# Attention followed by an MLP on one core: engine orders searched with another rule for ties between GpSimd's masks and VectorE's 16-bit sums

## The chip, the cores and the metric

The kernel runs on one core of a Trainium2 chip. A core has four compute engines that matter here: TensorE (PE, matmuls), VectorE (DVE), ScalarE (ACT) and GpSimd (POOL); SyncE (SP) issues transfers. Each engine works through its own list of instructions in order and waits on semaphores for the others. The metric is the device time in microseconds (us) of one execution; the figure for a kernel is the median of several runs.

## The reference

Attention with a few extra "beacon" keys that every query may see, then an MLP with a gated activation:

```python
B, H, S, Nb, D = 8, 8, 576, 16, 64
k_all = concat([beacon_k, k], axis=2)            # 592 keys
scores = q @ k_all.T / sqrt(D)                   # per batch and head
scores[causal] = -1e9                            # beacon keys are never masked
a = exp(scores - max); a /= a.sum(-1) + 1e-9
x = (a @ v_all).transpose(0, 2, 1, 3).reshape(4608, 512)
h = x @ w_in                                     # 512 -> 2048
out = (h * sigmoid(1.702 * h)) @ w_out           # 2048 -> 512, float32
```

## The kernel before

**Attention.** The 64 pairs of batch and head are worked in 16 sets of four heads, two sets to a batch. The score matrix is computed transposed, keys on the partitions, and only where the causal mask leaves something. It is cut into 60 chunks of up to 512 columns for four heads at once, so that a chunk fills four PSUM banks. For chunk i, the operation `qk` of the plan (L571 for sets 0 to 7, whose queries and keys are transposed by DVE; L560 for sets 8 to 15, whose transposed copies come by a transposing DMA from a staged 16-bit copy, L489 and L493) makes the scores; `exp` (L583, ACT) writes their exponentials as 16-bit numbers into E. There is one score tile, so chunk i+1 waits for the exponentials of chunk i. `mask` (L601, POOL, `affine_select`; for the first sets some of them on DVE, L594) zeroes the part of a block above the diagonal. `zadd` (L619, DVE, 16-bit sums) adds the key blocks of E up into zs, from which PE forms the softmax denominators with a matmul by ones. `av` (L659, PE) are the matmuls of attention: the first index after the set says which half of the head dimension is formed, 2 stands for the denominators. `z1` and `z2` (L669, L675, L680, DVE) transpose the denominators and invert them, `norm` (L697, DVE) multiplies and writes x, transposed, into xT.

**MLP.** Its tokens go in ten groups, two of 256 and eight of 512. The first layer is `m1` (L721), or, for some groups, a fast scheme with seven products instead of eight, whose pieces `f` (L926) are combined by ACT (`seed` L936, `keep7` L942) and DVE (`sum` L945) and activated at L951. The second layer is plain (`m2`, L767, copied from PSUM by `evac`, L780) for the first two groups; from group 2 on it is also a scheme of seven products (L839), with sums of its right sides on DVE in 16 bit (`s`, through a helper, L787), `half` (ACT, L852) and `join` (DVE, L855) behind it, and stores on SP (L863, L870). The weights' own sums (wsum, t, in SF and tB) and those of x (xsum, in tiles that the profile names sig) also run through L787. All these 16-bit sums are DVE instructions that read E, x, weights or activations from SBUF.

**Order.** Nothing about the order is found at run time. The program first lists about 1,740 operations with their dependencies. A literal table ORDER then gives for each engine the sequence of its operations, by number, and a literal list BANK the PSUM bank of each tile, in the order in which the tiles are first named. PSUM has eight banks: four form a ring that av, m1, m2, f and the products share; the other four hold the score tile or, in the phases between, more of the ring's tiles. A tile may open in a bank only when the operations that close the bank's last tile (norm, gelu, evac, half, join and their like) are done.

`Plan.run` (from L184) walks these lists: at each step it looks at the first operation left of every engine, works out from estimated durations and latencies when it could start, and takes the earliest. The result is the order in which instructions are emitted to the program; the sequence on each engine is that of ORDER in any case. The plan models that DVE's 16-bit sums and POOL's masks use a shared port: an operation carries port 1 (a DVE operation whose name is in HELD: s, zadd, xsum, wsum, t, mask, bk) or port 2 (a POOL mask), and does not start before the planned end of the last operation with the other port:

```python
                if o.port:
                    t = max(t, held[3 - o.port])
                if first is None or t < first[0]:
                    first = t, e, i
```

Engines are looked at in the order PE, ACT, DVE, POOL, SP, so that with equal starts DVE's sum is placed before POOL's mask, and the mask is then held behind it.

ORDER and BANK were made outside of this program, by a search over such plans. At the start PE runs warm-up matmuls (L1525) while the first loads arrive.

Of the kernel before, what the change touches and what calls it, by code (L numbers as in the profile page):

```python
# [18 lines left out]
        126, 136, 162, 165, 235, 129, 147, 131, 150, 152, 240, 168, 171, 242, 249, 174, 194, 245, 177, 197, 266,  # L19
        200, 203, 206, 209, 275, 256, 212, 215, 254, 277, 284, 252, 259, 261, 287, 280, 180, 225, 181, 226, 416,  # L20
        291, 289, 227, 294, 296, 419, 182, 187, 183, 422, 228, 188, 189, 190, 429, 320, 302, 310, 316, 308, 328,
        306, 332, 314, 304, 322, 318, 312, 324, 326, 330, 342, 343, 438, 447, 218, 219, 220, 221, 450, 351, 352,
        353, 344, 367, 476, 362, 345, 368, 363, 369, 364, 618, 370, 372, 373, 354, 374, 365, 621, 375, 441, 445,
        486, 443, 627, 386, 387, 491, 493, 646, 489, 388, 389, 503, 379, 648, 380, 381, 505, 382, 507, 519, 535,
        541, 509, 525, 537, 511, 539, 512, 515, 543, 544, 521, 523, 547, 553, 527, 557, 528, 531, 551, 555, 576,
        567, 568, 651, 637, 577, 578, 569, 579, 570, 592, 593, 816, 597, 598, 587, 594, 588, 819, 589, 590, 595,
        599, 660, 822, 640, 644, 642, 665, 830, 604, 605, 600, 663, 667, 848, 606, 607, 611, 673, 612, 851, 613,
        614, 677, 679, 882, 681, 682, 675, 685, 689, 695, 711, 705, 727, 709, 707, 723, 713, 714, 721, 693, 691,
        717, 839, 697, 698, 725, 746, 701, 737, 747, 748, 1020, 892, 844, 738, 739, 740, 749, 757, 758, 1023,
        842, 846, 897, 899, 895, 1030, 759, 762, 774, 775, 763, 1049, 776, 767, 764, 768, 760, 1051, 765, 769,  # L30
        770, 777, 905, 1054, 781, 907, 782, 783, 909, 921, 937, 784, 911, 955, 923, 925, 913, 914, 941, 939,
        927, 930, 929, 943, 917, 946, 945, 933, 957, 949, 959, 953, 969, 970, 971, 1219, 1063, 1040, 972, 989,
        978, 979, 980, 990, 981, 1222, 991, 992, 1045, 1043, 1066, 1225, 1068, 1070, 1047, 994, 1233, 995, 996,
        997, 1076, 999, 1251, 1000, 1001, 1002, 1006, 1007, 1254, 1013, 1008, 1009, 1014, 1080, 1285, 1078,
        1015, 1084, 1016, 1085, 1092, 1082, 1124, 1108, 1094, 1096, 1110, 1088, 1112, 1098, 1114, 1128, 1101,
        1100, 1116, 1117, 1126, 1104, 1120, 1295, 1242, 1130, 1149, 1140, 1141, 1431, 1142, 1150, 1151, 1245,
        1249, 1152, 1143, 1434, 1247, 1300, 1302, 1298, 1441, 1160, 1161, 1162, 1163, 1165, 1460, 1166, 1177,
        1178, 1167, 1170, 1462, 1168, 1179, 1171, 1172, 1308, 1173, 1465, 1180, 1310, 1184, 1312, 1185, 1324,
        1186, 1187, 1340, 1314, 1326, 1328, 1342, 1330, 1316, 1317, 1356, 1344, 1320, 1332, 1333, 1358, 1360,
        1451, 1474, 1336, 1365, 1364, 1362, 1346, 1454, 1456, 1349, 1348, 1368, 1458, 1479, 1481, 1477, 1352,  # L40
        1380, 1381, 1487, 1503, 1389, 1390, 1489, 1391, 1505, 1491, 1507, 1382, 1392, 1509, 1511, 1383, 1495,
        1512, 1493, 1400, 1515, 1496, 1405, 1406, 1407, 1519, 1401, 1499, 1535, 1402, 1525, 1408, 1403, 1521,
        1523, 1539, 1537, 1410, 1411, 1527, 1412, 1413, 1528, 1531, 1541, 1543, 1559, 1568, 1569, 1560, 1544,
        1570, 1547, 1417, 1561, 1424, 1425, 1614, 1426, 1630, 1418, 1419, 1618, 1420, 1634, 1427, 1632, 1616,
        1596, 1562, 1579, 1597, 1580, 1598, 1571, 1599, 1581, 1638, 1582, 1636, 1623, 1584, 1585, 1620, 1639,
        1642, 1586, 1622, 1589, 1646, 1590, 1587, 1591, 1626, 1592, 1662, 1650, 1648, 1603, 1604, 1666, 1668,
        1605, 1606, 1652, 1654, 1664, 1655, 1670, 1671, 1658, 1686, 1674, 1687, 1695, 1696, 1706, 1688, 1689,
        1711, 1697, 1712, 1716, 1713, 1698, 1714, 1707, 1708, 1709, 1717, 1718, 1719, 1720, 1725, 1726, 1727,
# [4 lines left out]
        172, 243, 175, 246, 178, 195, 198, 267, 201, 204, 207, 210, 276, 213, 216, 278, 281, 417, 420, 184, 423,  # L53
        191, 431, 430, 229, 303, 311, 317, 333, 309, 329, 321, 315, 307, 305, 319, 313, 323, 325, 327, 331, 448,
        222, 451, 478, 477, 350, 619, 622, 628, 629, 647, 504, 649, 506, 536, 508, 510, 538, 542, 540, 514, 520,
        526, 516, 522, 524, 546, 548, 554, 550, 518, 530, 532, 558, 552, 534, 556, 652, 575, 817, 820, 823, 832,
        831, 849, 674, 852, 678, 680, 884, 883, 684, 686, 706, 676, 688, 712, 710, 708, 728, 690, 696, 716, 720,
        694, 722, 718, 724, 692, 700, 704, 726, 702, 1021, 745, 1024, 1031, 1032, 1050, 1052, 906, 1055, 908,
        922, 938, 910, 956, 912, 924, 926, 916, 940, 928, 942, 920, 944, 932, 918, 936, 934, 958, 952, 948, 950,
        960, 954, 1220, 977, 1223, 1226, 1234, 1235, 1252, 1077, 1255, 1081, 1286, 1287, 1079, 1093, 1083, 1109,  # L60
        1125, 1087, 1111, 1089, 1095, 1097, 1113, 1099, 1129, 1115, 1091, 1107, 1103, 1127, 1121, 1119, 1123,
        1105, 1131, 1432, 1148, 1435, 1442, 1443, 1461, 1463, 1309, 1466, 1311, 1325, 1341, 1315, 1313, 1327,
        1343, 1331, 1329, 1319, 1357, 1321, 1323, 1335, 1361, 1359, 1337, 1339, 1363, 1345, 1347, 1367, 1351,
        1355, 1369, 1488, 1353, 1504, 1490, 1371, 1506, 1492, 1508, 1510, 1388, 1494, 1514, 1518, 1516, 1498,
        1500, 1536, 1520, 1522, 1526, 1524, 1538, 1540, 1530, 1502, 1534, 1542, 1532, 1550, 1546, 1548, 1615,
        1631, 1617, 1633, 1619, 1635, 1567, 1637, 1621, 1641, 1643, 1629, 1645, 1647, 1663, 1627, 1625, 1651,
        1649, 1667, 1653, 1669, 1657, 1665, 1661, 1659, 1677, 1675, 1673, 1694, 1743,
# [3 lines left out]
        232, 233, 127, 157, 128, 161, 164, 130, 148, 167, 413, 149, 132, 151, 153, 170, 263, 250, 173, 265, 264,  # L71
        176, 179, 196, 251, 199, 202, 205, 208, 257, 211, 258, 214, 255, 285, 253, 217, 286, 262, 415, 414, 288,
        260, 426, 292, 290, 293, 297, 495, 427, 295, 298, 428, 496, 434, 497, 299, 300, 435, 475, 436, 335, 437,
        334, 339, 336, 340, 338, 439, 337, 624, 347, 473, 474, 341, 440, 301, 346, 355, 348, 356, 482, 626, 349,
        625, 483, 484, 359, 366, 371, 485, 442, 376, 487, 488, 444, 357, 358, 492, 494, 446, 490, 499, 390, 500,
        501, 502, 498, 383, 513, 633, 545, 517, 656, 549, 529, 634, 533, 561, 635, 559, 565, 636, 563, 560, 564,
        562, 638, 571, 573, 566, 582, 639, 584, 574, 572, 657, 658, 659, 591, 596, 661, 662, 641, 581, 645, 666,
        643, 580, 601, 668, 664, 669, 583, 608, 670, 671, 672, 615, 888, 683, 835, 836, 687, 837, 838, 729, 733,
        715, 719, 889, 840, 699, 703, 890, 891, 841, 732, 730, 734, 731, 735, 741, 893, 845, 742, 894, 754, 843,
        743, 847, 750, 751, 898, 896, 1036, 900, 901, 902, 736, 744, 752, 761, 753, 766, 771, 778, 903, 904,  # L80
        1059, 1037, 785, 1060, 915, 919, 931, 935, 951, 947, 1061, 961, 962, 965, 1038, 966, 963, 967, 1039,
        1062, 973, 964, 968, 1041, 976, 974, 975, 1042, 1064, 986, 1065, 993, 1067, 1044, 982, 1046, 1071, 984,
        1072, 985, 1069, 1073, 983, 1074, 998, 1075, 1048, 1003, 1238, 1010, 1239, 1017, 1240, 1291, 1086, 1241,
        1090, 1292, 1293, 1294, 1106, 1102, 1118, 1122, 1132, 1243, 1244, 1136, 1133, 1134, 1135, 1296, 1137,
        1297, 1144, 1138, 1250, 1145, 1246, 1154, 1157, 1139, 1146, 1248, 1299, 1147, 1156, 1304, 1447, 1303,
        1164, 1155, 1305, 1301, 1306, 1448, 1449, 1307, 1169, 1174, 1153, 1181, 1450, 1188, 1470, 1471, 1318,
        1472, 1473, 1322, 1334, 1338, 1372, 1452, 1453, 1475, 1476, 1366, 1455, 1457, 1350, 1376, 1373, 1459,
        1480, 1354, 1478, 1370, 1483, 1374, 1484, 1485, 1486, 1384, 1393, 1482, 1375, 1378, 1379, 1377, 1513,
# [1473 lines left out]
```

## Time and profile before

| | |
|---|---|
| median of 3 runs | 320.81 us (320.31 to 320.88) |
| profiled execution | 321.22 us |
| its span, from the first to the last instruction | 319.4 us |
| mean granted TensorE clock in the span | 0.997 |
| moved by DMA | 33.51 MB in 112522 packets |

How to read the profile's lines: an instruction group has a line number of the program, an engine, the operation, the tile written and the tile read with partitions x elements, the count after an x, the busy time and the mean of one in ns, and then the idle time of the engine just ahead of the group with what ended it. A row of the timeline has start, duration, engine, line, operation, tiles and count; several like instructions in a row stand as one with their count, and a bracket tells how long the engine was idle before. The duration of a row of matmuls holds the modelled drain of the last one, so rows of PE overlap by some tenths, and the price of a matmul is read from start to start. A row of the windows has the stretch, its length, and for each engine the busy time in it. In the waits, "PE s L560 <- DMA qT<-qD: 0.6, 1, 0.6" means that PE, at line 560 on tile s, waited 0.6 us in total, once, and at most 0.6, for that transfer.

### The profile page before, as it was taken

Reading aid. Unit: us, or ns where it says so; the run is one execution under the profiler, and the core shown is the slowest. Engines: PE = TensorE matmul, PEld = TensorE weight load, DVE = VectorE, ACT = ScalarE, POOL = GpSimd, SP = SyncE. Lnnn points to the kernel's source line nnn. Section 1 sums busy time; section 2 is a strip of 40 time slices with the busy share of each in tenths; the row PEclk is TensorE's granted clock in tenths of the full one; section 3 lists DMA queues with packets and bytes.
Section 4 is the critical chain, followed back from the end, with each engine's and each line's share of the span. In section 5 each row is a group of like instructions: output and inputs, shape, how many; then the busy total and the mean of one; then the engine's idle time right before and its main releaser. Section 6 shows DMA issues by size and latency. Waiting matters only on the chain.

```text
span 319.4 us, 9295 instructions
## 1 busy us (share of the span) xinstructions
PE 309.9 (97%) x3947; PEld 232.2 (73%) x3947; DVE 255.3 (80%) x497; ACT 231.9 (73%) x309; POOL 136.7 (43%) x186
## 2 busy tenths in 40 slices
PE   6999999999999999989999999999999999999994
PEld 2567774445777777767778777777788888888884
DVE  5777988795999589897998799689958984776773
ACT  1778884677758987699869986898779687544820
POOL 8769558791848902595368204830350000000000
PEclk9999999999999999999999999999999999999998
DMA  7999999999999994599299903990036000120202
GB/s 122 178 202 191 147 192 168 138 190 95 88 87 111 192 108 92 112 159 161 17 129 151 203 0 44 155 152 30 3 23 146 2 3 2 66 68 34 101 33 101
DMA packets 112522, 33.51 MB, mean 105 GB/s; under 512 B 97504, under 2 KB 109920, under 8 KB 112480
## 3 DMA queue, kind: packets, MB, share of 16 engines
q0 software_dynamic: 83008, 18.55, 66.4%
q1 hardware_dynamic: 29264, 14.28, 19.4%
q8 instruction: 31, 0.51, 0.7%
q14 instruction: 11, 0.09, 0.1%
q10 hardware_dynamic: 208, 0.07, 0.1%
HBM read 37.22 MB, written 14.22 MB: 161 GB/s over the span
## 4 chain that ended last, share of the span: by engine, by line
PE 88%; ACT 5%; DVE 2%; DMA 2%; issue 1%; SPq 0%; DVEq 0%; ACTq 0%
PE u L839 29%; PE u L926 20%; PE u L721 13%; PE u L659 9%; PE u L767 4%; PE s L571 4%; PE s L560 4%; PE u L1525 4%; ACT E L583 2%; DMA qT<-qD 2%; PE p L571 1%; DVE osb L855 1%; ACT g L951 1%; ACT L951 1%; ACT u L936 1%
## 5 line engine op out<-in xcount | busy, mean ns | idle before, releaser
L583 ACT ACTIVATE E<-s 128x2048 f16<-128x2048 f32 (+3 forms) x59 | 90.7, 1553 | 31.7 <-PE s L560 16.0
L601 POOL TENSOR_SCALAR_AFFINE_SELECT E<-E 128x512 f16<-128x512 f16 (+3 forms) x78 | 62.5, 887 | 101.6 <-ACT E L583 86.1
L839 PEld LDWEIGHTS <-g 128*128 128x128 f16 x768 | 72.7, 98 | 11.8 <-issue 0.5
L839 PE MATMUL u<-w,g 128*128 128x256 f16 x512 | 67.2, 273 | 0.0
L951 ACT ACTIVATE g<-u 128x512 f16<-128x512 f32 x96 | 53.3, 628 | 12.4 <-DVE u L945 8.5
L855 DVE SCALAR_TENSOR_TENSOR osb<-u,osb 128x512 f32<-128x512 f32 (+2 forms) x51 | 33.2, 656 | 18.5 <-PE u L839 16.3
L721 PE MATMUL u<-xT,w 128*128 128x256 f16 (+1 forms) x256 | 45.4, 326 | 0.5 <-ACT g L951 0.5
L926 PEld LDWEIGHTS <-SF 128*128 128x128 f16 x384 | 37.2, 98 | 6.5 <-issue 0.3
L926 PE MATMUL u<-sig,SF 128*128 128x256 f16 x288 | 40.1, 273 | 0.0
L721 PEld LDWEIGHTS <-w 128*128 128x128 f16 x256 | 24.2, 98 | 15.1 <-issue 1.2
L839 PE MATMUL u<-tB,g 128*128 128x256 f16 x256 | 34.8, 273 | 0.0
L475 POOL DMA_DIRECT2D vb<-in_v_dram x32 | 33.1, 1118 | 0.0
L926 PEld LDWEIGHTS <-w 128*128 128x128 f16 x288 | 28.0, 98 | 5.3 <-issue 0.7
L936 ACT ACTIVATE u<-u 128x512 f32<-128x512 f32 x48 | 27.9, 596 | 3.8 <-PE u L926 3.1
L697 DVE TENSOR_TENSOR xT<-u,rz 128x352 f16<-128x352 f32 (+6 forms) x58 | 26.3, 478 | 3.9 <-PE u L659 3.5
L787 DVE TENSOR_TENSOR g<-g 128x512 f16<-128x512 f16 x64 | 28.1, 454 | 1.6 <-PE u L839 0.9
L926 PE MATMUL u<-xT,w 128*128 128x256 f16 x192 | 28.1, 272 | 0.3 <-ACT E L583 0.2
L659 PE MATMUL u<-E,vb 128*32 128x352 f16 (+8 forms) x928 | 27.7, 263 | 0.3 <-DVE xT L697 0.2
L659 PEld LDWEIGHTS <-vb 128*32 128x32 f16 (+1 forms) x928 | 20.4, 96 | 7.2 <-issue 3.6
L619 DVE TENSOR_TENSOR zs<-zs,E 128x1344 f16<-128x1344 f16 (+2 forms) x36 | 23.8, 662 | 1.4 <-POOL E L601 0.4
L945 DVE TENSOR_TENSOR u<-u,kn 128x512 f32<-128x512 f32 x24 | 16.0, 694 | 6.8 <-ACT kn L942 3.5
L945 DVE TENSOR_TENSOR u<-u,qn 128x512 f32<-128x512 f32 x24 | 16.1, 695 | 6.5 <-PE u L926 5.3
(72 smaller groups left out, 449.3 us busy)
## 6 DMA issues: line engine op xcount, KB each, us to landing
out_dram<-osb SPq DMA_DIRECT2D x35, 256.0 KB, 3.0
vb<-in_v_dram POOLq DMA_DIRECT2D x24, 128.0 KB, 5.6
kn<-in_k_dram POOLq DMA_DIRECT2D x8, 288.0 KB, 7.3
qn<-in_q_dram POOLq DMA_DIRECT2D x8, 288.0 KB, 6.7
qD<-in_q_dram POOLq DMA_DIRECT2D x8, 288.0 KB, 6.4
kD<-in_k_dram POOLq DMA_DIRECT2D x8, 288.0 KB, 8.1
w<-in_moe_w_in_dram POOLq DMA_DIRECT2D x8, 256.0 KB, 8.5
w<-in_moe_w_out_dram POOLq DMA_DIRECT2D x4, 512.0 KB, 9.5
```

The lines of the kernel that those rows point to most:

```text
L475: nc.gpsimd.dma_start(out=t[0 : hi - lo, j, h0:h1, :], in_=v[b, h0:h1, lo:hi, :].rearrange("h n d -> n h d"),)
L583: nc.scalar.activation(out=Es[s][:, h0:h1, c0:c1], in_=sall[(i, p)][:, :, o : o + c1 - c0], func=AFT.Exp, scale=0.125,)
L601: nc.gpsimd.affine_select(out=blk, in_=blk, compare_op=ALU.is_ge, fill=0.0, base=off + (Nb if j == 0 else 0), pattern=[[0, Q], [1, w]], ch ...
L659: nc.tensor.matmul(u[32 * h : 32 * h + 32, a:e], lhs, src[0:kw, h, col : col + e - a], start=first, stop=last, skip_group_check=s >= EARLY ...
L721: nc.tensor.matmul(u[:, o + a - t0 : o + e - t0], w1t[:, kp, nt * P : (nt + 1) * P], xT[:, kp, a % XR : (e - 1) % XR + 1], start=(kp == 0 ...
L787: (nc.vector if eng == "DVE" else nc.gpsimd).tensor_tensor(out=out, in0=a, in1=b, op=op)
L839: nc.tensor.matmul(u[:, HM * mt : HM * (mt + 1)], lhs[:, n, mt * P : (mt + 1) * P], rhs[:, n, :], start=(n == 0 and (mt == 0 or apart) and ...
L855: nc.vector.scalar_tensor_tensor(out=osbs[(g, dst)][:, c0:c1], in0=rings[("p", g, p)][:, c0:c1], scalar=scale_of(g), in1=osbs[(g, src)][:, ...
L926: nc.tensor.matmul(u[:, HM * n : HM * (n + 1)], lhs[x][:, (2 * i + n) * P : (2 * i + n + 1) * P], rhs[:, x, :], start=fresh and n == 0 and ...
L936: nc.scalar.mul(out=ring_tile(dst)[:, :], in_=rings[src][:, :], mul=1.0)
L945: nc.vector.tensor_tensor(out=rings[dst][:, :], in0=rings[src][:, :], in1=p7s[(g, i)], op=ALU.add)
L951: nc.scalar.activation(out=gts[g][:, n : n + 2, HM * h : HM * (h + 1)], in_=rings[src][:, :].rearrange("p (n w) -> p n w", n=2), func=AFT. ...
```

## The change

One condition in `Plan.run` is new: where a POOL operation could start at the very moment that another engine's could, it is taken first. And the tables ORDER and BANK are replaced by ones that a search found with this rule in its plan. No instruction is added, removed or changed in shape. Of the operations in the plan, these stand at another place in their engine's list: PE 377 of 590, DVE 356 of 451, ACT 153 of 300, POOL 143 of 179, SP 39 of 71; the largest shifts are 35, 28, 17, 84 and 5 places. PE's list has 130 changes between kinds of matmul tile where it had 133; ACT's has the same 12 loads of a function table.

```diff
@@ Plan.run @@
                 if o.port:
                     t = max(t, held[3 - o.port])
-                if first is None or t < first[0]:
+                if first is None or t < first[0] or (t == first[0] and e == "POOL"):
                     first = t, e, i
@@ ORDER, some rows of PE's list (221 lines of tables in all) @@
-        126, 136, 162, 165, 235, 129, 147, 131, 150, 152, 240, 168, 171, 242, 249, 174, 194, 245, 177, 197, 266,
-        200, 203, 206, 209, 275, 256, 212, 215, 254, 277, 284, 252, 259, 261, 287, 280, 180, 225, 181, 226, 416,
...
+        126, 136, 162, 165, 235, 129, 147, 131, 150, 152, 240, 168, 171, 242, 174, 194, 245, 249, 177, 197, 266,
+        203, 200, 206, 209, 275, 256, 212, 215, 254, 277, 284, 252, 259, 261, 287, 289, 280, 225, 180, 181, 226,
...
```

In words, the places that the prediction speaks of. Score chunk 27 stands before a half of a product of group 2 (product 4) instead of after it. The value matmuls of set 7 stand directly behind chunk 32, ahead of two product pieces. On DVE, between the reciprocals of set 12 and its first norm stand twelve sums of activations instead of seven, and PE's value tiles of sets 12 and 13 take other banks. Two copies of the plain second layer (`evac`) stand on ACT ahead of two exponentials of sets 4 and 5, instead of one ahead of them and one behind. The last `zadd` of set 5 stands ahead of the last of three joins of group 2 instead of behind it. On ACT, two exponentials of sets 9 and 10 change places ahead of the activations of group 4. The new lists begin with the same sixteen PE operations as the old ones, and the last products, joins and stores stand in the same order.

188 rows, old and new, of tables (BANK, ORDER) are left out of this document.

## The prediction

> **What bounds the kernel now.** I read the page's head first, then the chain that ended last.
>
> ```profile
> span 319.4 us, 9295 instructions
> PE 309.9 (97%) x3947; PEld 232.2 (73%) x3947; DVE 255.3 (80%) x497; ACT 231.9 (73%) x309; POOL 136.7 (43%) x186
> PE 88%; ACT 5%; DVE 2%; DMA 2%; issue 1%; SPq 0%; DVEq 0%; ACTq 0%
> ```
>
> TensorE is busy 97% of the span and carries 88% of the chain. The change touches no duration, so the only stock it can draw on is the time in which PE does not run. The windows of 20 us say where that is (left out are five in which PE is busy for all 20.00 us, others up to 300, and one with 19.99).
>
> ```profile
> core 0: us, PE busy (x) PEld busy (x) DVE busy (x) ACT busy (x) POOL busy (x), PEclk, DMA share, GB/s
> 20.00:40.00 20.00, 19.24 (x391) 15.36 (x384) 17.01 (x34) 17.19 (x19) 14.00 (x23) 1.00 1.41 175
> ...
> 80.00:100.00 20.00, 19.69 (x356) 14.63 (x353) 19.34 (x34) 13.72 (x11) 13.03 (x14) 1.00 1.06 94
> 100.00:120.00 20.00, 19.89 (x200) 15.04 (x198) 15.23 (x31) 18.58 (x29) 11.83 (x13) 1.00 1.59 140
> 120.00:140.00 20.00, 19.64 (x297) 14.70 (x295) 17.95 (x36) 15.06 (x14) 10.66 (x16) 1.00 0.77 107
> 140.00:160.00 20.00, 19.30 (x256) 14.25 (x257) 17.23 (x34) 18.23 (x28) 10.77 (x12) 1.00 1.05 110
> ...
> 200.00:220.00 20.00, 19.37 (x190) 14.66 (x189) 15.43 (x24) 18.02 (x30) 8.84 (x12) 1.00 1.33 133
> ```
>
> Missing in them: 0.76 + 0.31 + 0.11 + 0.36 + 0.70 + 0.63 = 2.87 us. DVE is the next engine: 19.34 of 20 us at 80 to 100, so a reordering of DVE is what PE can feel. The waits name two of PE's idle stretches and the one large wait that stems from the masks:
>
> ```profile
> PE s L560 <- DMA qT<-qD: 0.6, 1, 0.6
> PE u L721 <- ACT g L951: 0.5, 1, 0.5
> DVE zs L619 <- POOL E L601: 2.3, 2, 1.9
> ```
>
> The masks cost DVE 2.3 us in two waits. Of PE's waits only the DMA one, 0.6 us, has nothing to do with the order on DVE or ACT: a transposed load lands late. Counted in the two lists, as many PE operations stand between the load's first possible moment and its user in the new order as in the old, so it stays.
>
> The ends do not move. The first sixteen PE operations, to about 21 us, are the same in both lists, and so are ACT's and DVE's there; the last products, joins and stores are the same too, so what lies behind PE's last work stays:
>
> ```profile
> 313.97 1.36 PE L839 MATMUL u<-w,g 128*128 128x256 f16 x11
> 315.89 0.83 SPq L870 DMA_DIRECT2D out_dram<-osb  x2
> ```
>
> PE ends at 313.97 + 1.36 = 315.33, the last stores are issued at 315.89, the span ends at 319.4.
>
> **The change, part by part.** All times below are in the profiled execution, 321.22 us, of which 319.4 is the span; it lies 0.41 above the median of the runs, 320.81, to which I add the sum at the end. 0.2% of it, 0.64 us, is about what a measurement can tell from no change.
>
> The one changed line of the planner emits nothing: it settles which engine is served first when a mask and a sum could start at the same planned moment. Each engine's list is written out, so the chip sees only the new lists and PSUM banks: 377 of 590 PE operations stand elsewhere in their list, 356 of 451 on DVE, 153 of 300 on ACT, 143 of 179 on POOL, 39 of 71 on SP. Number, kinds and ACT's table loads are equal. So I price places.
>
> First the premise, the masks:
>
> ```profile
> L601 POOL TENSOR_SCALAR_AFFINE_SELECT E<-E 128x512 f16<-128x512 f16 x42 | 37.7, 911 | 79.2 <-ACT E L583 63.7 <-issue 15.3
> L601 POOL TENSOR_SCALAR_AFFINE_SELECT E<-E x78: 357/637/3088, 17.1 to 239.7; 128x512 f16<-128x512 f16 x42, 128x320 f16<-128x320 f16 x20, 128x448 f16<-128x448 f16 x14, 128x192 f16<-128x192 f16 x2
> 60.16 1.20 POOL L601 TENSOR_SCALAR_AFFINE_SELECT E<-E 128x512 f16<-128x512 f16 x1 [2.35 <-ACT E L583]
> 60.19 1.71 DVE L787 TENSOR_TENSOR SF<-SF,w 128x1024 f16<-128x1024 f16 x2
> ...
> 203.35 1.33 DVE L619 TENSOR_TENSOR zs<-zs,E 128x1344 f16<-128x1344 f16 x1
> 203.93 1.20 POOL L601 TENSOR_SCALAR_AFFINE_SELECT E<-E 128x448 f16<-128x448 f16 x1
> ```
>
> A mask of the 512 form takes 911 ns on average where the median mask takes 637, and one took 3088: 42 x 0.27 = 11.5 us of stretching, next to 16-bit sums on DVE. At 60.16 a mask that waited during a sum ran before the next queued sum: the rule of the new plan. At 203.35 a sum begins while a first mask runs, and the second mask, queued behind it, takes 1.20 us, twice the median, and ends 0.45 after the sum: there the sum that had waited went ahead, the rule of the old plan. So the new rule describes some collisions better and others worse, and I give the better premise no gain of its own.
>
> By the Trainium skill, page "SBUF — State Buffer", section "Who interferes with whom", the port pair that DVE shares with GpSimd is an exclusive lock; an earlier section of the page gives it to whichever operation starts first, for the whole instruction. The two places above agree, and by that rule the plan that lets a mask pass a sum already waiting is wrong where the plan before was right; this is the last rival below.
>
> Switches of PE between kinds of matmul tile (scores, attention values, the rest): 133 in the old list, 130 in the new. The price from these rows, and the place of the next term:
>
> ```profile
> 98.05 1.88 ACT L583 ACTIVATE E<-s 128x2048 f16<-128x2048 f32 x1 [0.87 <-PE s L571]
> 99.21 0.60 PE L926 MATMUL u<-xT,w 128*128 128x256 f16 x4
> 99.65 0.60 PE L839 MATMUL u<-tB,g 128*128 128x256 f16 x4
> 100.18 0.63 PE L571 MATMUL s<-qT,kT 32*128 32x400 f16 x16
> ```
>
> Four equal matmuls take 99.65 - 99.21 = 0.44 us ahead of one of their kind and 100.18 - 99.65 = 0.53 ahead of scores, hence about 0.1 a switch; three fewer: **-0.3**.
>
> Chunk 27 of the scores (at 100.18) needs the score tile that the exponential of chunk 26 reads until 98.05 + 1.88 = 99.93. In the new order it stands ahead of the product at 99.65, so PE gets there at 99.65 and waits about **+0.28**; the product then runs behind it at no loss. Below nothing it cannot go, and if ACT is late by more, so is the wait.
>
> Attention values of set 7 (131.32 here):
>
> ```profile
> 128.87 1.69 DVE L697 TENSOR_TENSOR xT<-u,rz 128x96 f16<-128x96 f32 x6
> 129.91 1.05 PE L839 MATMUL u<-tB,g 128*128 128x256 f16 x8
> 131.32 0.92 PE L659 MATMUL u<-E,vb 128*32 128x224 f16 x28
> ```
>
> They now stand directly behind chunk 32 at 129.90, 131.32 - 129.90 = 1.42 us earlier. Their PSUM banks are freed by the norms of set 6, which end at 128.87 + 1.69 = 130.56. Priced 0 to 130.56 - 129.90 = 0.66; the new list also lets DVE take some of these norms earlier, so about half: **+0.3**.
>
> Sets 12 and 13:
>
> ```profile
> 219.51 1.08 DVE L787 TENSOR_TENSOR sA<-g 128x512 f16<-128x512 f16 x3
> 222.90 0.53 DVE L697 TENSOR_TENSOR xT<-u,rz 128x352 f16<-128x352 f32 x1
> 224.31 1.88 PE L659 MATMUL u<-E,vb 128*32 128x352 f16 x57
> ```
>
> Between the reciprocals of set 12 and its first norm (222.90) the old list has 7 sums of the products' right sides, the new one 12. A sum takes about 0.33 from start to start (the three at 219.51 reach 220.51), so the norm comes 5 x 0.33 = 1.65 later. PE's user of its bank started at 224.31, 224.31 - (222.90 + 0.53) = 0.88 after it. That leaves 1.65 - 0.88 = 0.77 at most; the new list, however, hands that user a bank freed by ACT and only later users the norm's, so 0 to 0.77, the middle: **+0.4**.
>
> The first layer of group 2:
>
> ```profile
> 61.72 0.60 ACT L780 ACTIVATE osb<-u 128x512 f32<-128x512 f32 x1 [1.63 <-PE u L767]
> 62.38 1.94 ACT L583 ACTIVATE E<-s 128x1536 f16<-128x1536 f32 x2
> ```
>
> Two copies from PSUM, 0.60 each, now both stand before the two exponentials of 62.38; in the old list the second follows them. The exponentials start about 0.5 later, the masks and sums behind them too, while the bank freed by the copy comes 0.5 sooner or more. The window from 60 to 80 us has no idle PE now, so little of either reaches it: between -0.2 and +0.3, **+0.1**.
>
> Denominators of set 5:
>
> ```profile
> 90.86 2.18 DVE L855 SCALAR_TENSOR_TENSOR osb<-u,osb 128x512 f32<-128x512 f32 x3
> 92.96 0.32 DVE L619 TENSOR_TENSOR zs<-zs,E 128x320 f16<-128x320 f16 x1
> 93.33 0.38 PE L659 MATMUL u<-zs,ones 128*32 128x288 f16 x8 [0.21 <-DVE zs L619]
> ```
>
> PE waits 0.21 for the last sum, which follows three joins. In the new list it is ahead of the last join: the wait goes, **-0.2**, and the join, 0.7 later, frees its bank for nobody near.
>
> ACT's order around groups 3 and 4 touches PE's 0.5 us behind the activation of L951: the two exponentials before it change places, and the sum behind which it stood has one DVE sum less ahead of it. But the table load before it stays where it is: 0 to -0.5, **-0.1**.
>
> SP's and POOL's transfers move by few places (39 of SP's 71, by at most 5). Their cover, PE's work between the score chunks, is the same, so nothing; uncovered, the row of 0.6 us above is the price of one.
>
> Sum: -0.3 + 0.28 + 0.3 + 0.4 + 0.1 - 0.2 - 0.1 = +0.48, taken as +0.5.
>
> **The rivals.** *Slower: the DVE order of sets 7 and 12 at its full price.* The banks come free at the old pace and PE stands at both: -0.3 + 0.28 + 0.66 + 0.77 + 0.3 = +1.7, none of the small gains: 322.5. It decides once the first norm of set 12 ends over 0.88 us later than now relative to PE. For it: DVE is the second busiest engine and the PE order is tight there. Against: the banks were dealt anew with that very order.
>
> *Faster: the new order closes idle stretches.* Of 2.87 us, 0.6 stays; half of the other 2.27 goes, with the switches: -1.1 - 0.3 = -1.4: 319.4. For it: every stretch but one hangs on DVE's or ACT's order. Against: the idle time lies in six pieces under 0.8 us, and the places that I can follow show as many new tight spots as old ones loosened.
>
> *Slower by the lock: whoever waited first goes on.* The new order counts on masks passing sums that the chip does not let pass. One more DVE wait like the longest of the waits above, 1.9 us, where PE needs the sum at once, as at 93.33: +1.9, 322.7. Against: 1.9 us of that wait cost PE nothing in the old order.
>
> *The change does nothing of its own.* That the rule only reshuffles ties and every move is covered gives -0.3 to 0, inside the first case's range.
>
> **How the numbers follow.** No change that can be told, at 320.81 + 0.5 = 321.3: 0.40, with its own range from 320.2 to 322.0 (the terms at their low ends, -0.3 + 0.28 - 0.2 - 0.2 - 0.5 = -0.9, seldom all at once; the high ends are the first rival); 0.08 of this lies above +0.64 and 0.03 below -0.64. Full price: 0.26. Faster: 0.26. Lock: 0.08. So faster 0.03 + 0.26 = 0.29, same 0.40 - 0.11 = 0.29, slower 0.08 + 0.26 + 0.08 = 0.42. The range for 8 in 10 reaches from 319.2, a little under the faster case, to 323.1, a little over the lock's: the faster case left out below 319.2 holds about 0.1, and so do the two slower ones above 323.1. The time is that of the likeliest case, **321.3**.
>
> **What would show it right or wrong.** Right: the score chunk near 99.9 waits about 0.3 us for ACT; the attention values of set 7 wait up to 0.66 for L697; a wait of PE for L697 at 223 to 227; no wait for the sum at 93.3; the DMA wait near 204 still 0.6. Wrong: windows from 20 to 220 us with under 1.5 us missing (faster), or any PE wait over 1 us for DVE (the lock or the full price), or a later first matmul or longer tail, which I hold equal.

## The result, and the profile after

The changed kernel took 319.63 us (median of 7 runs), the kernel before 320.90 beside it: a ratio of 0.9955 (95% interval 0.9940 to 0.9970). Run again later beside the kernel before it was 319.55 against 320.73: 0.9970 (0.9957 to 0.9983). It is faster, by 1.2 to 1.3 us between the medians, where the prediction had 0.5 us slower. The first profile of it fell in a slow execution, with a granted TensorE clock of 0.949, so the lines here are of a second profile of the same program at the full clock (319.32 us, first experiment).

The head of its page, with busy times and the shares of the chain:

```profile
span 317.6 us, 9305 instructions
PE 309.4 (97%) x3947; PEld 232.6 (73%) x3947; DVE 247.2 (78%) x497; ACT 232.9 (73%) x309; POOL 135.5 (43%) x186
PE 64%; ACT 3%; DVE 2%; issue 1%; DVEq 0%; ACTq 0%
```

PE's work is as long as it was (309.4 for 309.9), DVE's is 8 us shorter, and little of that reaches PE, as the windows of 20 us say, in the same columns and stretches as before. (Of the 8 us, 5 lie in the 16-bit sums of L787 and L619, whose records add up to 115.9 us for 121.1. So DVE's sums are stretched less under the new lists, whether by the new rule or not no run shows.)

```profile
20.00:40.00 20.00, 19.70 (x395) 15.76 (x388) 16.91 (x34) 18.01 (x21) 14.77 (x25) 1.00 1.32 164
...
80.00:100.00 20.00, 19.39 (x354) 13.95 (x356) 19.16 (x35) 13.92 (x12) 11.54 (x12) 1.00 1.26 111
100.00:120.00 20.00, 19.99 (x204) 15.51 (x192) 15.13 (x30) 18.93 (x30) 10.25 (x15) 1.00 0.98 112
120.00:140.00 20.00, 19.43 (x305) 14.69 (x294) 17.20 (x36) 15.17 (x14) 12.82 (x18) 1.00 0.84 125
140.00:160.00 20.00, 19.51 (x276) 14.43 (x277) 16.61 (x36) 17.79 (x27) 11.35 (x13) 1.00 1.53 129
...
200.00:220.00 20.00, 19.97 (x199) 15.03 (x197) 15.82 (x30) 18.07 (x30) 6.82 (x9) 1.00 0.45 80
```

These miss 0.30 + 0.61 + 0.01 + 0.57 + 0.49 + 0.03 = 2.01 us where before missed 2.87. The largest part of the difference is one stretch, 200 to 220: 0.03 for 0.63. The stretch from 20 to 40, with 0.30 for 0.76, holds a stall that differs from execution to execution (below), and the others trade with each other. A second part lies behind PE's last matmul, in the timelines of DVE and SP there. First before, then after:

```profile
315.37 0.82 DVE L855 SCALAR_TENSOR_TENSOR osb<-u,osb 128x128 f32<-128x128 f32 x3 [1.05 <-PE u L839]
```

```profile
312.13 1.91 PE L839 MATMUL u<-w,g 128*128 128x256 f16 x16
313.21 0.42 DVE L855 SCALAR_TENSOR_TENSOR osb<-u,osb 128x256 f32<-128x256 f32 x1 [0.18 <-PE u L839]
314.08 0.49 DVE L855 SCALAR_TENSOR_TENSOR osb<-u,osb 128x128 f32<-128x128 f32 x2 [0.45 <-PE u L839]
313.66 1.28 SPq L870 DMA_DIRECT2D out_dram<-osb  x2
```

Before, DVE does three joins after the last matmul: two of 128 columns, which need it, and then one of 256, which does not (the row of three carries the form of its first). After, the 256 columns are joined at 313.21, behind the matmuls of their own half, and their store goes out at 313.66; only the two small joins and their two stores follow the last matmul. From the last matmul's end (315.33 before, 312.13 + 1.91 = 314.04 after) to the end of the span it was 4.05 us and is 317.61 - 314.04 = 3.57.

To tell lasting differences from chance I took the starts of the score chunks from the traces of all profiles at the full clock. The first chunk itself starts at 8.5 to 9.4 us, and chunk 10 stands 22.7 us behind it in every one. Chunks 10 to 12 take 5.0 to 5.6 us, with a stall inside a matmul group that has no releaser in the records. Chunk 12 starts at 36.5 us in both profiles of the changed kernel and at 36.8 to 37.5 in the four of the kernel before; but four profiles of variants of the changed kernel, whose lists are the same up to there, have it at 36.7 to 37.3, so no lasting gain can be read from the start. Then come:

| stretch, us | before | after |
|---|---|---|
| chunk 12 to 47 | 163.67, 163.67, 163.64, 164.21 | 163.68, 163.66 |
| chunk 47 to 49 | 19.19, 18.81, 18.49, 18.61 | 18.51, 18.51 |
| chunk 49 to the last matmul | 95.48, 95.48, 95.47, 95.48 | 95.38, 95.38 |
| last matmul to the end | 4.05, 4.05, -, 4.05 | 3.57, 3.54 |

(Before: the first profile, the rule alone, the end alone, whose end is changed, and before again. After: the changed kernel again, and timed.) So all that moved on PE, DVE and ACT between chunks 12 and 47, and behind 49, is worth 0.1 us. What the changed kernel lastingly gains, as far as these rows tell, lies at chunk 48 and at the end.

### The profile page after: what moved, and what is told of

It is laid out like the page before. It is cut to its first block, busy times and chain, and to the rows that moved or that the text cites. A ratio compares the mean times of both kernels' runs of the same rounds, so it can differ in the third digit from the quotient of the medians.

```text
span 323.9 us, 9305 instructions
## 1 busy us (share of the span) xinstructions
PE 315.6 (97%) x3947; PEld 235.1 (73%) x3947; DVE 247.4 (76%) x497; ACT 233.5 (72%) x309; POOL 135.2 (42%) x186
## 4 chain that ended last, share of the span: by engine, by line
PE 65%; ACT 3%; DVE 2%; issue 0%; DVEq 0%
PE u L839 28%; PE u L926 22%; PE u L659 6%; PE u L721 5%; PE s L560 4%; ACT E L583 2%; DVE osb L855 1%; PE s L571 1%; ACT L951 0%; DVE xT L697 0%; ACT g L951 0%; DVE zs L619 0%; DVE rz L680 0%; ACT u L936 0%; ACT kn L942 0%
## 5 line engine op out<-in xcount | busy, mean ns | idle before, releaser
L601 POOL TENSOR_SCALAR_AFFINE_SELECT E<-E 128x512 f16<-128x512 f16 (+3 forms) x78 | 59.2, 849 | 105.5 <-ACT E L583 63.5
L839 PEld LDWEIGHTS <-g 128*128 128x128 f16 x768 | 74.2, 99 | 13.2 <-issue 0.9
L951 ACT ACTIVATE g<-u 128x512 f16<-128x512 f32 x96 | 54.0, 613 | 17.9 <-DVE u L945 9.1
L721 PE MATMUL u<-xT,w 128*128 128x256 f16 (+1 forms) x256 | 47.2, 334 | 0.4 <-ACT g L951 0.4
L926 PE MATMUL u<-sig,SF 128*128 128x256 f16 x288 | 40.9, 277 | 0.0
L721 PEld LDWEIGHTS <-w 128*128 128x128 f16 x256 | 24.6, 99 | 15.1 <-issue 0.8
L475 POOL DMA_DIRECT2D vb<-in_v_dram x32 | 35.3, 1127 | 0.7 <-issue 0.7
L926 PEld LDWEIGHTS <-w 128*128 128x128 f16 x288 | 28.4, 99 | 5.1 <-issue 0.6
L926 PE MATMUL u<-xT,w 128*128 128x256 f16 x192 | 28.9, 277 | 0.2 <-ACT E L583 0.2
L787 DVE TENSOR_TENSOR g<-g 128x512 f16<-128x512 f16 x64 | 26.7, 429 | 1.3 <-PE u L839 1.0
L619 DVE TENSOR_TENSOR zs<-zs,E 128x1344 f16<-128x1344 f16 (+2 forms) x36 | 22.9, 642 | 3.2 <-POOL E L601 2.9
```

Source lines behind the costliest of these rows:

```text
L475: nc.gpsimd.dma_start(out=t[0 : hi - lo, j, h0:h1, :], in_=v[b, h0:h1, lo:hi, :].rearrange("h n d -> n h d"),)
L601: nc.gpsimd.affine_select(out=blk, in_=blk, compare_op=ALU.is_ge, fill=0.0, base=off + (Nb if j == 0 else 0), pattern=[[0, Q], [1, w]], ch ...
L721: nc.tensor.matmul(u[:, o + a - t0 : o + e - t0], w1t[:, kp, nt * P : (nt + 1) * P], xT[:, kp, a % XR : (e - 1) % XR + 1], start=(kp == 0 ...
L787: (nc.vector if eng == "DVE" else nc.gpsimd).tensor_tensor(out=out, in0=a, in1=b, op=op)
L839: nc.tensor.matmul(u[:, HM * mt : HM * (mt + 1)], lhs[:, n, mt * P : (mt + 1) * P], rhs[:, n, :], start=(n == 0 and (mt == 0 or apart) and ...
L926: nc.tensor.matmul(u[:, HM * n : HM * (n + 1)], lhs[x][:, (2 * i + n) * P : (2 * i + n + 1) * P], rhs[:, x, :], start=fresh and n == 0 and ...
```

## The experiments

Where a line number of a profile below is two higher than in the listing, the tables of that variant are two rows longer; nothing else differs.

**The changed kernel again** (no edit).

> The changed kernel once more, for a profile at the full clock. Its undisturbed spans so far are 317.6 to 318.1 us, against 319.4 before, so 1.3 to 1.8 us have to be found in the rows. Theory (idle stretches closed): the windows from 20 to 220 us miss about 1.3 us in place of 2.87, and the transfer wait of 0.6 us at score chunk 48 is among what went. Rival (fewer switches of kind, less drain between kinds): the windows miss as much as before, and PE's work itself is shorter by over 0.8 us.

319.32 us, span 317.6: the first theory's windows are wrong by size (2.0 missed, not 1.3), the transfer wait has gone as it said, and the end, which neither named, has 0.48.

**The rule alone.**

```diff
-                if first is None or t < first[0]:
+                if first is None or t < first[0] or (t == first[0] and e == "POOL"):
```

> The kernel before with the new tie rule alone, its own lists and banks kept: each engine's list is the same, only the order in which the program is written out across engines changes. If the lists carry the whole gain: the time of before within 0.2%, 320.3 to 321.5 us. If the order of writing out matters (semaphores placed elsewhere): up to 1.3 us below it, 319.6 us.

320.34 us for 320.72, ratio 0.9994 (0.9984 to 1.0004). The order of writing out is worth nothing that shows, 0.5 us at the most by the interval; the lists carry the gain.

**The end alone**, in the kernel before.

```diff
 DVE, its last three:
-     join9[2nd half, cols 128-255], join9[2nd half, cols 0-127], join9[1st half]
+     join9[1st half], join9[2nd half, cols 128-255], join9[2nd half, cols 0-127]
 SP:
-     store9[2nd half], store9[1st half]
+     store9[1st half], store9[2nd half]
```

> The kernel before, with two operations moved: the join of the last tile's first half (256 columns, its matmuls end 0.87 us ahead of the last one) ahead of the two joins that wait for the last matmul, and its store ahead of the other one. Theory (the end of the program carries a part of the gain): from the last matmul to the end 3.57 us in place of 4.05, so 0.48 us faster, 320.2 us where before gives 320.7. Rival (the end is as long, since the last store's landing sets it): no change.

```profile
314.30 0.43 DVE L857 SCALAR_TENSOR_TENSOR osb<-u,osb 128x256 f32<-128x256 f32 x1 [0.18 <-PE u L841]
315.17 0.49 DVE L857 SCALAR_TENSOR_TENSOR osb<-u,osb 128x128 f32<-128x128 f32 x2 [0.45 <-PE u L841]
```

The large join stands ahead of the last two as in the changed kernel, and the end is 3.55 us long for 4.05. The time: 320.31 for 320.51, 0.9989 (0.9974 to 1.0004). The profile shows the 0.5, the times agree with it but cannot tell it from nothing by themselves.

**The loads out**, in the kernel before.

```diff
 POOL:
+     ldv6, ldv6, ldv6  directly behind the ldv6 at 176.6
      mask12, mask12, mask12,
-     ldv7, mask12, ldv6, mask12, ldv6, mask13, ... ldv6
+     mask12, mask12, mask13, ... ldv7 (at 208)
```

> The kernel before, with four value loads moved on POOL's queue: three of batch 6 up to 177 us, directly behind the one at 176.6, and one of batch 7 from 197.7 down to about 208, so that none is issued between 190 and 205. Theory (value loads beside the transposed load of queries stretch it): that load lands 3 to 3.5 us after its issue in place of 6.0 and 5.5, PE's wait of 0.3 to 0.6 us for it at about 204 goes, and the kernel is 0.3 to 0.7 us faster. Rival (the output stores on the same queue stretch it): the wait stays, no change.

The transfers issued between 190 and 205 us, with their median time to landing; before, then this variant:

```profile
vb<-in_v_dram POOLq DMA_DIRECT2D x3, 128.0 KB, 6.2
qT<-qD SPq DMA_TRANSPOSE x1, 6.0
```

```profile
out_dram<-osb SPq DMA_DIRECT2D x2, 256.0 KB, 2.7
qT<-qD SPq DMA_TRANSPOSE x1, 3.6
```

The transposed load takes 3.6 us for 6.0, with the two output stores still beside it, and PE no longer waits at chunk 48 (47 to 49 in 18.47). So the value loads stretch it and not the stores. The time stays: 320.50 for 320.51, 1.0000 (0.9988 to 1.0013), which misses the 0.3 to 0.7 us that the theory had. The profile has a reason for part of that. With the loads gone, four masks run in a row on POOL, and a sum on DVE that started just ahead of a mask before now meets one that was queued; before, then this variant:

```profile
198.59 0.41 DVE L787 TENSOR_TENSOR sig<-xT 128x512 f16<-128x512 f16 x1
```

```profile
196.80 2.82 POOL L603 TENSOR_SCALAR_AFFINE_SELECT E<-E 128x320 f16<-128x320 f16 x4 [0.96 <-ACT E L585]
199.06 0.83 DVE L789 TENSOR_TENSOR sig<-xT 128x512 f16<-128x512 f16 x1
```

The norm behind that sum, which PE needs, comes 0.4 us later, and PE loses 0.2 (chunk 36 to 47 in 47.79 for 47.59). And the wait that went is not there in each execution of the kernel before (below).

**The old end**, in the changed kernel: the edit of the end turned round.

> The changed kernel with the end as it was before: the join of the last tile's first half behind the two that wait for the last matmul, and its store last. Theory (the end carries 0.48): 0.48 us slower than the changed kernel, 320.1 us. Rival: 319.6 us, as the changed one.

```profile
314.87 0.82 DVE L857 SCALAR_TENSOR_TENSOR osb<-u,osb 128x128 f32<-128x128 f32 x3 [1.06 <-PE u L841]
315.39 0.82 SPq L872 DMA_DIRECT2D out_dram<-osb  x2
```

The three joins in a row are back and the end takes 4.02 us. 320.24 us; 0.9996 (0.9985 to 1.0006) of before, where the changed kernel, timed beside other runs of before, is at 0.9970. As the theory had it, within the intervals.

**The loads in**, in the changed kernel.

```diff
 POOL:
      mask12, mask12,
+     ldv7, ldv7, ldv7,
      mask13, ...
```

> The changed kernel with three value loads of batch 7 issued at 195.5 to 198.5 us, beside the transposed loads, in place of 207 to 229. Theory (loads beside it stretch the transposed load): PE waits 0.3 to 0.9 us at score chunk 48, 203 us, and the kernel is slower by as much, 319.9 to 320.5 us. Rival (what went there is the order on PE or DVE, or the stores): 319.6 us, no wait at 203.

> The changed kernel with the three value loads issued at 195.5 to 198.5 us, once more, for a second profile: its times fell in two halves, 319.5 to 319.8 and 320.2 to 320.7. Theory (the stretched transposed load is late in some executions): in an execution of the slow half PE waits 0.3 to 0.7 us at chunk 48, in one of the fast half none. Rival: the halves have another cause, at PE's other stalls, and chunk 48 does not wait in either.

The transposed load of queries, in the changed kernel and in the two profiles of this variant:

```profile
qT<-qD SPq DMA_TRANSPOSE x1, 3.2
```

```profile
qT<-qD SPq DMA_TRANSPOSE x1, 4.9
```

```profile
qT<-qD SPq DMA_TRANSPOSE x1, 4.7
```

It is stretched, by half, but PE waits at chunk 48 in neither profile (320.19 and 319.94 us): here the load has room for 4.9. The times are between, 320.0 us, 0.9986 (0.9974 to 0.9997) of before, and why they fell in two halves stays open. The first profile, of the slower half, has 0.36 us more from chunk 24 to 28 than the second (25.79 for 25.43), in a stall without a releaser, which speaks for the rival of the second run. So the stretching is shown both ways, and the wait only in one.

**Both edits in the kernel before.**

> The kernel before with the two edits together: the last tile's joins and stores in the changed order, and the four value loads off the transposed load's time. Theory (these two places carry nearly all, and what moved on PE is worth under 0.1): 0.49 at the end and 0.1 to 0.7 at score chunk 48, less 0.2 for a norm that comes late behind it, so 0.4 to 1.0 us faster than before, and 0.0 to 0.4 slower than the changed kernel run beside it. Rival (the reordering of PE, DVE and ACT as a whole carries the gain): over 0.6 us slower than the changed kernel.

320.20 for 320.73: 0.9987 (0.9974 to 0.9999), and 0.65 us behind the changed kernel beside it (319.55). The gain on before is in the theory's range; the distance to the changed kernel is not, and by the condition written ahead of the run it is the rival's (over 0.6 us). The profile: 3.56 us at the end, no wait at 48, 0.2 for the late norm, 0.1 behind chunk 49, and a first chunk at 9.04 for 8.54, which is chance as far as the rows tell. That makes 0.3 lasting of the 0.65, and some 0.1 more on average for the race at 136 us (below), which these lists still have. The executions of the two kernels put the distance at 0.4 to 0.9 us (95%, an estimate from their 12 and 11 times), so 0.4 is at its edge: that the two places carry nearly all of the gain is what the rows say, and the times do not show it.

**Three places mended**, in the changed kernel.

```diff
 PE:  f3.0.1,
-     qk27, m2.2.4.0,
+     m2.2.4.0, qk27,
 DVE:
-     s2.2.2 (ahead of turn7)             z2.7, norm6, norm6, norm6
+     s2.2.2 (behind the fourth join2)    norm6, norm6, norm6, z2.7
```

> The changed kernel with three places mended: score chunk 27 behind the first piece of product 4 again; one 16-bit sum (s, group 2) moved from ahead of set 7's turn to behind the fourth join, so that the last two denominator sums of set 5 and the join behind them come 0.34 us earlier; the reciprocal of set 7 behind the three norms of set 6. Theory (each place's wait on PE is its price): 0.23 + up to 0.43 + 0.33, so 0.6 to 1.0 us faster than the changed kernel. Rival (DVE is full there, what one operation gains the next loses): 0.2 us for chunk 27 alone, the other waits come back at most 1 us later.

```profile
PE u L659 <- DVE xT L697: 0.8, 1, 0.8
PE u L721 <- ACT g L951: 0.5, 1, 0.5
PE u L659 <- DVE osb L855: 0.3, 1, 0.3
```

Slower than the changed kernel by 0.9 us: 320.46 us, 0.9991 (0.9979 to 1.0004) of before. The three norms in a row save 0.41 from chunk 28 to 32 (12.36 for 12.77) and cost 1.03 from 32 to 36 (24.75 for 23.72): set 7's own norms now stand behind the reciprocal, and PE waits 0.8 for one of them. The wait for the join (osb) is unchanged. Chunk 27 no longer waits, but its exponential starts that much later, and a first-layer piece at 102 waits 0.29 for it instead. From chunk 24 to 28, with the moved sum also in it, it is 25.6 us for 25.4: the wait was the cheaper place. The rival was right about the direction and the loss went further than it said.

**The changed kernel, timed beside these.**

> The changed kernel on the same chip, as the measure for the other two: 319.3 to 319.8 us where before gives 320.5 to 320.9, with no wait at score chunk 48 and 3.57 us from the last matmul to the end. Rival (the end alone separates them): 320.1 us.

319.55 us for 320.73; 47 to 49 in 18.51, the end 3.54. These are the theory's numbers.

**The kernel before again** (no edit).

> The kernel before once more, for its profile. Theory (the transposed load beside three value loads lands 5.4 to 6.2 us after its issue and varies): PE waits 0.1 to 0.7 us at score chunk 48, and from the last matmul to the end are 4.05 us again. Rival (the wait was chance and not the loads): no wait, and the load lands in about 3.5 us with the value loads beside it.

```profile
qT<-qD SPq DMA_TRANSPOSE x1, 4.3
```

```profile
136.16 1.10 DVE L787 TENSOR_TENSOR sig<-xT 128x512 f16<-128x512 f16 x1
136.14 0.84 POOL L601 TENSOR_SCALAR_AFFINE_SELECT E<-E 128x320 f16<-128x320 f16 x1
137.32 0.60 PE L926 MATMUL u<-sig,SF 128*128 128x256 f16 x4 [0.32 <-DVE sig L787]
```

This time the load landed in 4.3 us, with the loads beside it, and PE did not wait. In the four profiles of the table, which have this order of loads, PE stood idle ahead of chunk 48 for 0.63, 0.34, 0.02 and 0 us, and chunks 47 to 49 took 0.27 us more on average than in the changed kernel. A fifth, the mask queued earlier (below), has no wait either. The traces hint at what decides: in the three profiles where the first value load was issued 0.2 to 0.5 us ahead of the transposed load, that one took 5.5 to 6.1 us; in the two where it was issued 0.1 to 0.2 us behind, 4.3. No run set this order, so it is a hint and not shown. In place of the wait at 48 another came, 0.5 us from 136.4 on (chunk 12 to 47 in 164.21). The same two instructions in the first profile of before:

```profile
136.34 0.41 DVE L787 TENSOR_TENSOR sig<-xT 128x512 f16<-128x512 f16 x1
136.33 0.85 POOL L601 TENSOR_SCALAR_AFFINE_SELECT E<-E 128x320 f16<-128x320 f16 x1
```

Mask and sum start within 10 to 20 ns of each other, the mask first by the record both times, and once the sum takes 0.41 us and once 1.10. This is the tie that the new rule is about, and on the chip it went one way and the other in the same program: of six profiles with these lists here, the sum took 0.41 us in five and 1.10 in one.

**A mask queued earlier**, in the kernel before, to decide that place.

```diff
 POOL:
-     mask9, ldv4, mask8, ldv4
+     mask9, mask8, ldv4, ldv4
```

> The kernel before with one mask of set 8 (136.3 us) ahead of the value load in front of it on POOL's queue, so that it stands ready behind the mask of 134.9 to 136.0 while two sums of x for group 4 are queued on DVE, the first of them waiting since 135.2. Theory (whoever has waited goes next): the first sum runs as before, then the mask, and the second sum takes 1.0 to 1.2 us in place of 0.41; PE waits 0.5 us for it at 136.4 and some 0.2 behind it, so 0.5 to 0.7 us slower in every execution, 321.0 to 321.4 us. Rival (DVE's sums keep the port while one is queued): the second sum 0.41 us, PE does not wait, 320.5 to 320.8 us.

```profile
134.91 1.75 POOL L601 TENSOR_SCALAR_AFFINE_SELECT E<-E 128x512 f16<-128x512 f16 x2
136.26 1.06 DVE L787 TENSOR_TENSOR sig<-xT 128x512 f16<-128x512 f16 x1
137.38 0.60 PE L926 MATMUL u<-sig,SF 128*128 128x256 f16 x4 [0.20 <-DVE sig L787]
```

321.21 us for 320.53: 1.0024 (1.0012 to 1.0036), slower by 0.7 us, with the sum at 1.06 in place of 0.41. The mask, which has waited, goes ahead of a sum queued behind another sum, and 0.65 us more of one sum on DVE become 0.45 between chunks 32 and 36 on PE (24.17 for 23.72). The loads out, above, show the same at a second place.

## Why the prediction was wrong

The sign was wrong because of one false premise and one incomplete one, both ahead of the sum, and a sum that was too high.

- **The ends do not move.** False. The text says, and so does the account of the change above it, that the last joins and stores stand in the same order. PE's list does; DVE's last three joins and SP's last two stores do not. I compared names, and these joins share one. It is worth 0.5 us: 4.05 to 3.55 us of the end, shown in both directions by the profiles of the end alone and the old end. In the trace of before the row of three joins 1.05 us behind an idle DVE, two of which alone needed the last matmul, was there to be read.
- **The transfer wait stays, since as much of PE stands in front.** The count was right and the step still failed: PE's cover is one side, and the load's own length the other. I held that at 6 us, and it is 3.2 to 3.7 where no value load runs beside it, and varies from 4.3 to 6.1 where some do. The prediction had "SP's and POOL's transfers move by few places" and counted SP's alone; on POOL the value loads of batches 6 and 7 moved by up to 21, and the new list issues none between 176 and 207 us. The gain is 0.3 us on average.
- **Switches, -0.3**: not tried alone, so the price stays unshown. **Chunk 27, +0.28**: right. The four matmuls ahead of it take 0.77 us to its start (98.93 to 99.70) where 0.53 was the price, a wait of 0.24, of which 0.17 shows as idle. But the wait hid an exponential that had to be late somewhere, as mending it showed.

```profile
98.93 0.60 PE L926 MATMUL u<-xT,w 128*128 128x256 f16 x4
99.70 0.64 PE L571 MATMUL s<-qT,kT 32*128 32x400 f16 x16 [0.17 <-ACT E L583]
```

- **Set 7, +0.3, sets 12 and 13, +0.4**: nothing. The timeline of DVE and PE after:

```profile
127.44 2.07 DVE L697 TENSOR_TENSOR xT<-u,rz 128x448 f16<-128x448 f32 x7
129.31 1.04 PE L659 MATMUL u<-E,vb 128*32 128x224 f16 x36
223.12 2.32 PE L659 MATMUL u<-E,vb 128*32 128x352 f16 x76
```

  The norms of set 6 now run in one row from 127.44, the last done at 129.0, ahead of PE's 129.31: the sum that stood between them had moved too. At 223.12 PE works on without a wait: the bank comes from ACT, as the text allowed at its lower end. I took the middle of two ranges whose lower ends the lists already held.
- **First layer of group 2, +0.1**: nothing; PE is busy for all of 60 to 80 us in both kernels.
- **Denominators of set 5, -0.2**: turned into another wait. The sum is early, and PE now waits 0.34 for the join:

```profile
93.06 0.38 PE L659 MATMUL u<-zs,ones 128*32 128x288 f16 x8 [0.34 <-DVE osb L855]
```

  "Frees its bank for nobody near" was the step that failed; that join frees the bank of this very tile.
- **ACT around group 4, -0.1**: the 0.5 us are unchanged. The price of 0 was right.
- **Sum**: +0.48 for what moved between the ends; measured -0.1 (the table). (In the windows of the prediction, those left out with PE busy for all 20.00 us are seven, not five; nothing hangs on it.)
- **The rivals.** The faster one has the right sign and size, 319.4, by the wrong road, so its number is luck: it halved the idle stretches by DVE's and ACT's order, while those stretches, but for the one of the transfer, nearly kept their sum (2.0 for 2.2 us), and the end and the transfer paid. The slower ones at DVE's full price did not come. The lock's rule, that who has waited goes first, held at the two places where a run put a mask in the queue (the queued mask, 1.06 us for 0.41, and the loads out, 0.83 for 0.41). By the Trainium skill's "SBUF — State Buffer", section "Who interferes with whom", issue order decides who blocks; the queued masks agree, while at 136 us the records have the mask 10 to 20 ns ahead in both profiles and the sum takes 0.41 in one and 1.10 in the other, so that they cannot tell. The rival's DVE wait did come, and more than it had: 6.3 us for 2.3.

```profile
DVE zs L619 <- POOL E L601: 6.3, 3, 3.3
```

  But PE waits for none of these sums in the profile after, so it cost the changed kernel nothing.

What stays open: 0.5 at the end, 0.3 at chunk 48 and 0.1 on PE make 0.9 of the 1.2 us, and the race at 136 us, which cost 0.5 in one profile of six, perhaps 0.1 more. Some 0.2 isn't placed, which is within the intervals of the times; and with both places edited the kernel before gained 0.53 us, under half of the 1.2, so that the rest stands on the rows of single profiles. That the rule in the search led to the new place of the value loads, by sending masks first, was not tried and cannot be read from a trace.

## What to carry to other kernels

Before a reordering is priced, compare what stands behind the last instruction of the bound engine, operation by operation and not by name: half a microsecond there counts in full, while 377 moved operations on the busiest engine came to 0.1. Price a transfer's wait from both sides, what covers it and what runs beside it. And a wait of the bound engine is only worth what the next wait leaves of it: mended together, three of them made the kernel 0.9 us slower.

## What the hardware showed besides

The warm-up matmuls do not end at a fixed time. Ten of them, in the profile of the end alone, and its window from 6 to 8 us, and then the same in the profile of both edits:

```profile
2.59 6.73 PE L1527 MATMUL u<-tB 128*128 128x512 f32 x10 [2.59 <-DVE tB L372]
```

```profile
6.00:8.00 2.00, 2.00 (x4) 0.80 (x3) 1.88 (x2) 0.00 (x0) 2.00 (x3) 1.00 1.13 201
```

```profile
2.59 5.42 PE L1525 MATMUL u<-tB 128*128 128x512 f32 x10 [2.59 <-DVE tB L370]
9.04 0.64 PE L571 MATMUL p<-qT,kT 32*128 32x288 f16 x24 [1.02 <-DVE qT L526]
```

They take 0.85 us each at first and half of that later. Over all profiles the pace changes within the matmul that starts at 5.3 us at the earliest and at 7.9 at the latest, 2.7 to 5.3 us behind the first one's start, while the profile's clock column says 1.00. In the first profile the ten hold PE until 9.25, past the data, in the second PE waits 1.02 for the data. The Trainium skill, "TensorE: Matmul & The Clock Gate", Part 1, has the window that opens the clock run freely, so that the point differs from run to run: the traces agree in that, but the page gives half a microsecond either way, and here the point moves over 2.6 us. It delays the first chunk by up to 0.8 us (9.42 in the second profile of the loads in, with the data there at 8.55), more than most of the differences sought here, and is the reason why stretches were compared and not only spans.
